# Block-causal attention with a gated feed-forward: low parts of q and k on another engine, scores and transposes in another order

## The chip, the cores and the metric

The kernel runs on one core of a Trainium2 chip. The metric is the device time of one execution in microseconds (us). Five engines work side by side, each through its own queue in order: TensorE (PE in the profile: matmuls and transposes, with weight loads shown as PEld), VectorE (DVE), ScalarE (ACT), GpSimd (POOL) and SyncE (SP, which issues DMAs).

## The reference

```python
def _attn_ref(q, k, v):                      # q, k, v: (8, 8, 576, 64)
    scores = scale * np.matmul(q, k.transpose(0, 1, 3, 2))
    mask = block_i >= block_j                # blocks of 64 positions
    scores = np.where(mask, scores, -1000000000.0)
    scores = scores - np.max(scores, axis=-1, keepdims=True)
    attn = np.exp(scores)
    attn = attn / (np.sum(attn, axis=-1, keepdims=True) + 1e-09)
    return np.matmul(attn, v)

def _moe_ref(x, w_in, g_ln, w_sg, b_sg, w_out):   # x: (8, 576, 512), the heads side by side
    h = gelu_tanh(x @ w_in)                  # w_in: 512 x 1024
    u, v = h[..., :512], h[..., 512:]
    v_n = (v - mean(v)) / np.sqrt(var(v) + 1e-06) * g_ln
    v_s = np.einsum('ts,bsd->btd', w_sg, v_n) + b_sg[None, :, None]
    return x + (u * v_s) @ w_out             # w_out: 512 x 512
```

Matmuls are made in near-fp32 precision from two parts of each operand, a high and a low one (`hi` is the value in the PE's shorter fp32 form, `lo` is the value less `hi`): hi x hi + hi x lo + lo x hi.

## The kernel before

The 64 heads of 8 batches are taken as 32 pairs. One *slot* (the function `slot`, lines 743 to 806) belongs to one pair n: it makes the attention values of pair n and, interleaved with them, the scores of pair n+1, so that the softmax of the next pair runs on DVE and ACT while PE does something else. Four slots make a batch.

In a slot PE does, in this order before the change: the transposes of the probabilities of pair n (tiles `pa`, `pb`, `pc`, `pd`, by the methods `turn0`, `turn2` with `turn2_rest`, `turn1` with `turn1_rest`, and `turn_first`), each two banks (one for each head) and each followed by a copy to SBUF as `pt` (by ACT or DVE); the score matmuls of pair n+1 in four steps (`step1` to `step4`, tile `s`, hereafter s1 to s4), each followed on DVE by a masked maximum of every row (`negm`; the instruction that applies the mask writes `prob` and accumulates the maximum) and on ACT by the exponentials (`exponents`); the matmuls of probabilities by values (`av0`, `av2`, `av1`, tile `ob`); and `turn_sums`, the transposes of the reciprocal sums `rx` to `pd` and `pe`, by which `normalise` multiplies (`x`). `split` cuts x into high and low parts (`xh` on DVE, `xl` and a tail on POOL). The reciprocal sums come from `inverse` at the head of a slot: `ri` on DVE, then `rx` on POOL.

In the seven places `hole(g[0])` to `hole(g[6])` of a slot stand *groups* of the feed-forward of an earlier batch: 5 of `accv`, 8 of `accu`, 8 of `accs` and 8 of `acco`, 29 for a batch, each one accumulation in one bank. Slots 0 to 3 have none, since no batch is complete. The table `FIRST` (line 741) says for slots 4 to 7 how many groups each place gets, `PLAN` (line 739) for all later slots.

PSUM has 8 banks in two pools, which are handed out in rotation: five for `s`, `ob` and the groups (`sbank`), three for the transposes (`pbank`). A tile can be written only when the reader of the bank's former tile is done: a `pa` follows the former `pd` or `pe`, a group follows an `s` that the maxima have read.

Inputs come a slot or two ahead. `load_qk` fetches q and k of pair n+2 by two DMAs; `split_qk` (lines 127 to 135), called near the end of slot n, cuts them in two: one cast on DVE (`qk_h`, 128x1152), then two subtractions on POOL (`qk_l`, 128x576 each). All these tiles have one buffer. Weights arrive as float64 and are made to high and low parts in small steps (`weight_step`; `load_weight`, lines 220 to 241, keeps `AHEAD` DMAs under way): each step has three operations on DVE (`w`), two on ACT and one on POOL (`wi_l`, `wo_l`). The table `WS` (line 731) says how many steps each of the slots 0 to 8 gets; a part that is needed earlier is pulled in by `need`.

Only PE's order is that of the program text inside slots. On the other engines the scheduler of the framework orders instructions by its own estimate when operands and buffers will be free, and each engine then works through that order.

The lines that the change touches are printed below with the functions that hold them.

Of the kernel before, what the change touches and what calls it, by code (L numbers as in the profile page):

```python
# [9 lines left out]
F32 = mybir.dt.float32  # L10
# [4 lines left out]
ALU = mybir.AluOpType  # L15
# [13 lines left out]
def kernel(  # L29
# [13 lines left out]
    B, H, D, S = qT.shape  # L43
    P = 128
    BLK = 64
    DM = H * D
# [22 lines left out]
    def page(dtype, n, name):  # L69
        tag, bufs = KINDS.get(name, KINDS["w"])  # L70
        return sp.tile([P, n], dtype, tag=tag, name=name, bufs=bufs)

    def bank(tag, name, bufs):
        return psum.tile([P, 512], F32, tag=tag, name=name, bufs=bufs)

    def sbank(name):
        return bank("s", name, 5)

    def pbank(name):
        return bank("p", name, 3)  # L80
# [22 lines left out]
    V, A, G, SP = Pinned(nc.vector, "V"), Pinned(nc.scalar, "A"), Pinned(nc.gpsimd, "G"), Pinned(nc.sync, "S")  # L103
# [23 lines left out]
    def split_qk(n):  # L127
        t = qk[n]
        hi = sp.tile([P, 2, S], F32R, tag="qk_h", name="qk_h", bufs=1)
        lo = sp.tile([P, 2, S], F32R, tag="qk_l", name="qk_l", bufs=1)  # L130
        V.tensor_copy(hi, t)
        for i in (1, 0):
            G.tensor_tensor(lo[:, i, :], t[:, i, :], hi[:, i, :].bitcast(F32), op=ALU.subtract)
        q_h, k_h, q_l, k_l = hi[:, 0, :], hi[:, 1, :], lo[:, 0, :], lo[:, 1, :]
        qk[n] = [(q_h, k_h), (q_h, k_l), (q_l, k_h)]

# [16 lines left out]
    t = sbank("warm")  # L153
# [15 lines left out]
    for s in (0, 1):  # L169
        t = cp.tile([P, NT, 2 * D], F32, name=f"v_f{s}")  # L170
# [5 lines left out]
    for s in range(4):  # L176
        row = []
        for i in range(NT):
            t = cp.tile([P, P * (i + 1) if i else BLK], F32, name=f"prob{s}_{i}")
# [8 lines left out]
    wo_h = cp.tile([P, NC, DM], F32R, name="wo_h")  # L188
    wo_l = cp.tile([P, NC, DM], F32R, name="wo_l")
# [5 lines left out]
    def split_weight(x, dh, dl):  # L195
        A.copy(dh, x)
        G.tensor_tensor(dl, x, dh.bitcast(F32), op=ALU.subtract)

    def from_f64(raw, dh, dl):

        n = raw.shape[-1]
        words = raw.bitcast(U32).rearrange("p (n t) -> p n t", t=2)
        hi, lo = words[:, :, 1], words[:, :, 0]
        tm = page(U32, 2 * n, "w")
        t, m = tm[:, :n], tm[:, n:]

        A.mul(m.bitcast(F32), hi.bitcast(F32), 2.0**-112)

        V.tensor_scalar(t, lo, 29, None, op0=ALU.logical_shift_right)
        V.scalar_tensor_tensor(
            t, hi, 0x80000000, t, op0=ALU.bitwise_and, op1=ALU.bitwise_or
        )
        V.scalar_tensor_tensor(
            t, m, 3, t, op0=ALU.logical_shift_left, op1=ALU.bitwise_or
        )
        split_weight(t.bitcast(F32), dh, dl)

    def load_weight(src, cols, dh, dl):  # L220

        W, AHEAD = 256, 4
        parts = [(c, slice(f, f + W)) for f in range(cols.start, cols.stop, W) for c in range(NC)]
        raws = {}

        def fetch(k):
            if k < len(parts):
                c, fs = parts[k]
                raws[k] = page(src.dtype, W, "raw")
                SP.dma_start(raws[k], src[c * P : (c + 1) * P, fs])  # L230

        for k in range(AHEAD):
            fetch(k)
        for k, (c, fs) in enumerate(parts):
            args = (raws.pop(k), dh[:, c, fs], dl[:, c, fs])
            if src.dtype == F32:
                split_weight(*args)
            else:
                from_f64(*args)
            fetch(k + AHEAD)  # L240
            yield True
# [26 lines left out]
    def load_gains():  # L268
# [10 lines left out]
            ("u0", load_weight(w_in, slice(0, DH // 2), wi_h, wi_l)),  # L279
            ("u2", load_weight(w_in, slice(DH // 2, DH), wi_h, wi_l)),  # L280
            ("s", load_spatial()),
            ("o", load_weight(w_out, slice(0, DM), wo_h, wo_l)),
        ]
    )

    def weight_step():

        with ExitStack() as stack:
            for ins in newest.values():
                stack.enter_context(tc.issue_after(ins.ins))  # L290
            while weights and next(weights[0][1], None) is None:
                weights.popleft()
# [96 lines left out]
    class Values:  # L389
# [15 lines left out]
            pt = self.pt[a, j] = sp.tile([P, 512], F32, tag="pt", name="pt", bufs=4)  # L405
            copy(TE[a, j], pt, t)

        def turn0(self, a):

            t = pbank("pa")  # L410
            for i in (4, 3, 2, 1):
                self.turn(a, t[:, (i - 1) * P : i * P], i, 0)
            self.out(a, 0, t)

        def turn2(self):

# [99 lines left out]
    def run_side(k):  # L516

        while k > 0 and side and side[0][0] != "G":
            k -= 1
            side.popleft()[1]()  # L520

    def run_gelu():

        if side and side[0][0] == "G":
            side.popleft()[1]()
# [196 lines left out]
    def hole(k=1):  # L722

        while k > 0 and work:
            try:
                next(work[0])
                k -= 1
            except StopIteration:
                work.popleft()

    WS = [2, 2, 2, 1, 10, 3, 3, 3, 2]

    def load_share(n, k):

        if n < len(WS):
            for _ in range(WS[n] * (k + 1) // 4 - WS[n] * k // 4):
                weight_step()

    PLAN = ["1111111", "1111111", "1111111", "1111112"]

    FIRST = ["1111111", "1111101", "0011011", "1011010"]

    def slot(n, sc):
        va = Values(n, sc)
        nx = Scores(n + 1) if n + 1 < N else None
        g = [int(x) for x in (FIRST if n // 4 == 1 else PLAN)[n % 4]]
        if n + 2 < N:
            load_qk(n + 2)
        if n + 1 < N:
            load_v(n + 1)  # L750
        va.inverse()
        va.turn0(0)
        va.turn0(1)
        hole(g[0])
        load_share(n, 0)
        run_side(2)

        va.turn2()
        va.turn2_rest()
        if nx:  # L760
            nx.step1()
            nx.step2()
        va.av0()
        if nx:
            nx.exponents(1, 4)
        hole(g[1])
        load_share(n, 1)
        run_side(2)
        hole(g[2])
        run_side(2)  # L770
        va.turn1()
        va.turn1_rest()
        va.turn_first()
        if nx:
            nx.step3()
            nx.step4()
        va.av2()
        if nx:
            nx.exponents(3, 0, 2)
        hole(g[3])  # L780
        load_share(n, 2)
        run_side(2)
        va.av1()
        va.av00()
        va.turn_sums()
        hole(g[4])
        va.normalise()

        wait = n // (H // 2) > 0 and n % (H // 2) < 2
        pending.append(va.split)  # L790
        if not wait:
            while pending:
                pending.popleft()()
        run_side(2)
        if n + 2 < N:
            split_qk(n + 2)
        load_share(n, 3)
        hole(g[5])
        run_gelu()
        run_side(3)  # L800
        hole(g[6])
        run_side(3)
        if n % (H // 2) == 1:
            while pending:
                pending.popleft()()
        return nx
# [75 lines left out]
```

## Time and profile before

| | before |
|---|---|
| three runs | 792.67, 793.02 and 795.04 us |
| profiled execution | 792.86 us, span 791.0 us |
| PE busy | 757.9 us (96%) |
| DVE busy | 495.5 us (63%) |
| ACT busy | 450.6 us (57%) |
| POOL busy | 272.4 us (34%) |
| mean granted PE clock | 0.985 |

The span is the time from the first to the last recorded instruction. A busy PE is not PE at its peak: the table of stretches further down also lists the granted clock, which is below full speed in the first 100 us. Rows of the timeline read: start, duration, engine, line, operation, written tile <- read tiles, shape, and, in brackets, the idle time of the engine before it with the instruction that ended it. Rows of the waits read: who waited for whom, total us, times, longest.

Where things lie: slot 0 starts at 10.6 us, slot 4 (the first with groups) at 70.9, slot 8 at 166.4, slot 9 at 192.3. From slot 8 on the four slots of a batch take 92.9 us.

### The profile page before, as it was taken

The page shows a single profiled execution, that of the slowest core. Times are in us where ns is not written, and L with a number is a line of the kernel's source. Part 1 is how long each engine was busy: PE and PEld are TensorE (multiplying, and loading weights), DVE is VectorE, ACT ScalarE, POOL GpSimd, SP SyncE. Part 2 cuts the span into 40 slices and gives each one's busy share as a digit, 9 for nine tenths or more (in the row PEclk, how much of TensorE's full clock was granted, in tenths as well). Part 3 has the DMA queues.
Part 4 walks back from the last instruction along what each step waited for, and adds up shares of the span by engine and source line. Part 5 has one row for each costly group of instructions (what it writes and reads, how often), then busy time and mean ns, then how long its engine had stood idle before and what let it go on. Part 6 is the DMA issues. An engine that isn't in the chain of part 4 may idle for free.

```text
span 791.0 us, 15794 instructions
## 1 busy us (share of the span) xinstructions
PE 757.9 (96%) x5926; PEld 640.4 (81%) x5926; DVE 495.5 (63%) x1457; ACT 450.6 (57%) x1172; POOL 272.4 (34%) x331
## 2 busy tenths in 40 slices
PE   7876998999999999999999999999999999999998
PEld 5554786878888888887888888888888978888998
DVE  5888679985866467654866548564676647633532
ACT  4775688567854478435973368544793358721600
POOL 4354265552424124351133414332243510422121
PEclk9989899999999999999999999999999999999999
DMA  7224324212241024311142122410233101320032
GB/s 231 70 92 145 96 91 140 88 61 75 76 150 61 1 76 121 106 60 38 39 136 90 61 75 61 132 65 31 76 107 120 60 7 71 105 76 31 1 120 75
DMA packets 46911, 65.66 MB, mean 83 GB/s; under 512 B 4082, under 2 KB 22514, under 8 KB 46836
## 3 DMA queue, kind: packets, MB, share of 16 engines
q1 hardware_dynamic: 46836, 64.67, 25.5%
q8 instruction: 46, 0.75, 0.4%
q14 instruction: 29, 0.24, 0.1%
HBM read 45.78 MB, written 18.87 MB: 82 GB/s over the span
## 4 chain that ended last, share of the span: by engine, by line
PE 77%; DVE 12%; ACT 8%; issue 1%; SPq 1%; DMA 1%; POOL 1%; DVEq 0%; POOLq 0%; ACTq 0%
PE accs L88 14%; PE acco L88 13%; PE accv L88 13%; PE ob L88 9%; PE s L88 8%; PE accu L88 8%; PE pc L91 3%; PE pb L91 3%; DVE bs L101 3%; ACT prob L101 3%; PE pa L91 2%; DVE w L101 2%; ACT L101 1%; DVE prob L101 1%; PE pe L91 1%; DVE pt L101 1%
## 5 line engine op out<-in xcount | busy, mean ns | idle before, releaser
L101 ACT ACTIVATE prob<-prob,negm 128x448 f32<-128x448 f32 (+4 forms) x320 | 176.3, 554 | 44.1 <-DVE negm L101 41.4
L101 POOL TENSOR_TENSOR qk_l<-qk_f,qk_h 128x576 fp32r<-128x576 f32 x62 | 91.9, 1502 | 231.6 <-issue 98.9
L101 DVE CUSTOM_DVE_ANT_0 prob<-s,mask 128x288 f32<-128x288 f32 (+2 forms) x320 | 117.0, 421 | 64.6 <-PE s L88 64.6
L88 PE MATMUL ob<-pt,v_f 128*64 128x512 f32 (+4 forms) x640 | 105.7, 443 | 0.9 <-ACT pt L101 0.8
L101 POOL TENSOR_TENSOR gl<-u,gh 128x288 fp32r<-128x288 f32 x64 | 51.8, 810 | 108.5 <-DVE gh L101 71.2
L88 PE MATMUL s<-qk_h 64*128 64x288 f32 (+1 forms) x372 | 87.4, 341 | 0.4 <-ACT u L101 0.4
L88 PE MATMUL accu<-xh,wi_h 128*128 128x288 f32 x256 | 78.1, 305 | 5.1 <-DVE negm L101 5.1
L88 PE MATMUL s<-qk_l,qk_h 64*128 64x288 f32 (+1 forms) x372 | 82.2, 302 | 0.0
L88 PE MATMUL accs<-ws_h,vh 128*128 128x288 f32 x256 | 78.2, 305 | 1.5 <-DVE negm L101 1.5
L88 PE MATMUL s<-qk_h,qk_l 64*128 64x288 f32 (+1 forms) x372 | 77.9, 299 | 0.0
L88 PE MATMUL acco<-gh,wo_h 128*128 128x288 f32 x256 | 77.7, 303 | 0.0
L88 PE MATMUL accs<-ws_h,vl 128*128 128x288 f32 x256 | 75.6, 295 | 0.0
L88 PE MATMUL accs<-ws_l,vh 128*128 128x288 f32 x256 | 75.5, 295 | 0.0
L88 PE MATMUL accu<-xl,wi_h 128*128 128x288 f32 x256 | 75.5, 295 | 0.0
L88 PE MATMUL accu<-xh,wi_l 128*128 128x288 f32 x256 | 75.4, 295 | 0.0
L88 PE MATMUL acco<-gl,wo_h 128*128 128x288 f32 x256 | 75.4, 294 | 0.0
L88 PE MATMUL acco<-gh,wo_l 128*128 128x288 f32 x256 | 75.4, 294 | 0.0
L88 PEld LDWEIGHTS ob<-pt,v_f 128*64 128x64 f32 x640 | 38.2, 137 | 42.0 <-issue 29.4
L88 PE MATMUL accv<-wi_h,xh 128*128 128x512 f32 x160 | 66.0, 413 | 3.8 <-POOL xh L101 3.8
L88 PEld LDWEIGHTS s<-qk_h 64*128 64x128 f32 x372 | 64.0, 188 | 1.4 <-ACT u L101 0.6
L101 DVE TENSOR_TENSOR u<-accs,u 128x288 f32<-128x288 f32 x64 | 29.2, 456 | 55.4 <-PE accs L88 55.3
L88 PEld LDWEIGHTS s<-qk_h,qk_l 64*128 64x128 f32 x372 | 63.8, 187 | 0.0
(104 smaller groups left out, 1954.6 us busy)
## 6 DMA issues: line engine op xcount, KB each, us to landing
spill<-x SPq DMA_DIRECT2D x32, 288.0 KB, 3.8
xr<-spill SPq DMA_DIRECT2D x32, 288.0 KB, 3.3
out_T<-xr SPq DMA_DIRECT2D x32, 288.0 KB, 3.3
qk_f<-in_qT SPq DMA_DIRECT2D x31, 288.0 KB, 3.2
qk_f<-in_kT SPq DMA_DIRECT2D x31, 288.0 KB, 3.8
v_f<-in_v SPq DMA_DIRECT2D x32, 256.0 KB, 3.1
raw<-in_w_in SPq DMA_DIRECT2D x16, 256.0 KB, 4.8
raw<-in_w_out SPq DMA_DIRECT2D x8, 256.0 KB, 4.8
```

The source lines that it names most:

```text
L88: return pin(nc.tensor.matmul(*a, **k), "P")
L91: return pin(nc.tensor.transpose(out, in_, identity), "P")
L101: return lambda *a, **k: pin(f(*a, **k), self.letter)
```

## The change

1. `split_qk`: the low parts are made on DVE, by one subtraction of 128x1152 instead of two of 128x576 on POOL.
2. `turn0`: both heads' `pa` tiles are taken together, and the transposes of block row 2 of both heads, which the exponentials finish last, come after those of block rows 4, 3 and 1.
3. In the first four slots (`early`), s1 and s2 and the first value matmuls (`av0`) come right behind `pa`, and `pb` (`turn2`) after them.
4. `turn1`, the whole-array transposes of `pc`, moves from behind the groups g[1] and g[2] to right behind `av0`; its small transposes (`turn1_rest`) stay.
5. `turn_sums` moves from the slot's end to right behind `av2`, ahead of the group g[3].
6. The tables: `WS` moves weight steps from slots 4, 6 and 7 to slots 5 and 8; `w_out` keeps 2 DMAs under way instead of 4; `FIRST` moves a group from the head of slot 4 to slot 5.

```diff
     hi = sp.tile([P, 2, S], F32R, tag="qk_h", name="qk_h", bufs=1)
     lo = sp.tile([P, 2, S], F32R, tag="qk_l", name="qk_l", bufs=1)
     V.tensor_copy(hi, t)
-    for i in (1, 0):
-        G.tensor_tensor(lo[:, i, :], t[:, i, :], hi[:, i, :].bitcast(F32), op=ALU.subtract)
+    V.tensor_tensor(lo, t, hi.bitcast(F32), op=ALU.subtract)
...
-    def load_weight(src, cols, dh, dl):
-        W, AHEAD = 256, 4
+    def load_weight(src, cols, dh, dl, AHEAD=4):
+        W = 256
...
-            ("o", load_weight(w_out, slice(0, DM), wo_h, wo_l)),
+            ("o", load_weight(w_out, slice(0, DM), wo_h, wo_l, 2)),
...
-        def turn0(self, a):
-            t = pbank("pa")
-            for i in (4, 3, 2, 1):
-                self.turn(a, t[:, (i - 1) * P : i * P], i, 0)
-            self.out(a, 0, t)
+        def turn0(self):
+            t = [pbank("pa"), pbank("pa")]
+            for tiles in ((4, 3, 1), (2,)):
+                for a in (0, 1):
+                    for i in tiles:
+                        self.turn(a, t[a][:, (i - 1) * P : i * P], i, 0)
+            for a in (0, 1):
+                self.out(a, 0, t[a])
...
-    WS = [2, 2, 2, 1, 10, 3, 3, 3, 2]
+    WS = [2, 2, 2, 1, 8, 5, 0, 0, 8]
...
-    FIRST = ["1111111", "1111101", "0011011", "1011010"]
+    FIRST = ["0111111", "1111111", "0011011", "1011010"]
...
-        va.turn0(0)
-        va.turn0(1)
+        va.turn0()
         hole(g[0])
...
-        va.turn2()
-        va.turn2_rest()
+        early = n < H // 2
+        if not early:
+            va.turn2()
+            va.turn2_rest()
         if nx:
             nx.step1()
             nx.step2()
         va.av0()
+        if early:
+            va.turn2()
+            va.turn2_rest()
         if nx:
             nx.exponents(1, 4)
+        va.turn1()
         hole(g[1])
...
         hole(g[2])
         run_side(2)
-        va.turn1()
         va.turn1_rest()
         va.turn_first()
...
         va.av2()
+        va.turn_sums()
         if nx:
             nx.exponents(3, 0, 2)
         hole(g[3])
...
         va.av1()
         va.av00()
-        va.turn_sums()
         hole(g[4])
         va.normalise()
```

Three places show what this does to the engines' orders. The first is PE in slot 0, from the first transposes on. In this piece of the difference the rows with - are those of before, those with + of the change (`prob_4` is block row 4 of the probabilities; the same sequence comes in slots 1 to 3).

```order
 L91 MATMUL pa<-ident,prob_4_116 128x128
 L91 MATMUL pa<-ident,prob_3_114 128x128
-L91 MATMUL pa<-ident,prob_2_112 128x128
 L91 MATMUL pa<-ident,prob_1_110 128x128
 L91 MATMUL pa<-ident,prob_4_125 128x128
 L91 MATMUL pa<-ident,prob_3_123 128x128
+L91 MATMUL pa<-ident,prob_1_119 128x128
+L91 MATMUL pa<-ident,prob_2_112 128x128
 L91 MATMUL pa<-ident,prob_2_121 128x128
-L91 MATMUL pa<-ident,prob_1_119 128x128
+L88 MATMUL s<-qk_h 128x288 x2
+L88 MATMUL s<-qk_l,qk_h 128x288 x2
```

Block row 2 of both heads moves to the end of `pa`, and the first score matmuls of the next pair follow at once, where ten `pb` transposes stood.

The second place is DVE between slots 0 and 1, from the cast of q and k (pair 2) to the first maxima of the next scores. Before:

```order
L101 CAST qk_h<-qk_f 128x1152
L101 TENSOR_SCALAR w<-raw 128x256
L101 SCALAR_TENSOR_TENSOR w<-raw,w 128x256
L101 TENSOR_TENSOR ri<-sums,tiny 128x10
L101 RECIPROCAL ri<-ri 128x10
L101 SCALAR_TENSOR_TENSOR w<-w 128x256
L101 TENSOR_TENSOR x<-pe,x 128x512
L101 TENSOR_TENSOR x<-pd,x 128x64
L101 CAST xh<-x 128x576
L101 COPY pt<-pa 128x512
L101 COPY pt<-pb 128x512
L101 ISA prob_4_116,negm<-s,mask 128x288
```

The same place after the change:

```order
L101 CAST qk_h<-qk_f 128x1152
L101 TENSOR_SCALAR w<-raw 128x256
L101 TENSOR_TENSOR qk_l<-qk_f,qk_h 128x1152
L101 SCALAR_TENSOR_TENSOR w<-raw,w 128x256
L101 TENSOR_TENSOR ri<-sums,tiny 128x10
L101 TENSOR_TENSOR x<-pe,x 128x512
L101 SCALAR_TENSOR_TENSOR w<-w 128x256
L101 TENSOR_TENSOR x<-pd,x 128x64
L101 RECIPROCAL ri<-ri 128x10
L101 CAST xh<-x 128x576
L101 COPY pt<-pa 128x512
L101 ISA prob_4_116,negm<-s,mask 128x288
```

`qk_l` stands third, ahead of the multiply by `pe`, and the copy of `pb` is no longer ahead of the first maxima.

The third place is PE in slot 9, around `av0` (the row `ob`). Before, then after the change:

```order
L88 MATMUL s<-qk_h,qk_l 128x288 x2
L88 MATMUL ob<-pt,v_f_105 64x512 x2
L88 MATMUL accu<-xh,wi_h 128x288
L88 MATMUL accu<-xl,wi_h 128x288
L88 MATMUL accu<-xh,wi_l 128x288
```

```order
L88 MATMUL ob<-pt,v_f_105 64x512 x2
L91 MATMUL pc<-ident,prob_4_134 128x128
L91 MATMUL pc<-ident,prob_3_132 128x128
L91 MATMUL pc<-ident,prob_2_130 128x128
L91 MATMUL pc<-ident,prob_4_143 128x128
L91 MATMUL pc<-ident,prob_3_141 128x128
L91 MATMUL pc<-ident,prob_2_139 128x128
L88 MATMUL accu<-xh,wi_h 128x288
```

Six whole-array transposes now stand between `ob` and the first matmul of the group; in the same way five (`pd`, four `pe`) stand between the `ob` of `av2` and the next group.

## The prediction

> **What bounds the kernel now.** The page comes first: which engine is busy, and at what clock.
>
> ```profile
> PE 757.9 (96%) x5926; PEld 640.4 (81%) x5926; DVE 495.5 (63%) x1457; ACT 450.6 (57%) x1172; POOL 272.4 (34%) x331
> PEclk9989899999999999999999999999999999999999
> ```
>
> TensorE (PE) is busy 757.9 of 791.0 us, and the diff leaves its matmuls and transposes the same in number. So an edit can win only from the 33.1 us in which PE stands still (and from clock), and can lose without limit. The second step is to see where the 33.1 us lie, with the busy time in stretches (after the span: PE, weight load, DVE, ACT, POOL, then granted clock, DMA share, GB/s).
>
> ```profile
> 0.00:20.00 20.00, 15.59 (x87) 11.48 (x88) 10.80 (x38) 9.37 (x27) 8.54 (x39) 0.91 0.70 232
> 20.00:40.00 20.00, 16.29 (x139) 11.13 (x138) 17.16 (x62) 15.04 (x48) 7.69 (x10) 0.91 0.21 66
> 40.00:60.00 20.00, 15.08 (x118) 10.27 (x114) 16.82 (x46) 13.54 (x45) 10.57 (x13) 0.83 0.33 99
> 60.00:80.00 20.00, 13.24 (x102) 9.38 (x103) 16.00 (x47) 11.16 (x34) 9.90 (x13) 0.89 0.44 141
> 80.00:100.00 20.00, 20.00 (x124) 14.64 (x124) 13.19 (x44) 13.48 (x38) 6.08 (x6) 0.85 0.26 89
> 100.00:120.00 20.00, 18.88 (x151) 16.14 (x151) 14.60 (x38) 16.97 (x37) 10.77 (x12) 1.00 0.29 90
> 120.00:140.00 20.00, 16.63 (x147) 13.40 (x143) 18.11 (x43) 17.87 (x44) 11.89 (x11) 1.00 0.43 139
> 140.00:160.00 20.00, 19.07 (x167) 16.13 (x165) 18.07 (x51) 11.12 (x35) 11.82 (x14) 1.00 0.29 86
> ```
>
> Of the idle time 19.8 us stand in the first 80 us (slots 0 to 3 and the opening of slot 4, where there are no feed-forward groups yet) and 5.4 us in 100 to 160 (slots 5 to 7). VectorE (DVE) is busy 80 to 86% from 20 to 80 us and 90% from 120 to 160, against 63% over the span. The third step is what ends PE's idle time, over the whole span:
>
> ```profile
> PE pa L91 <- ACT pt L101: 6.6, 4, 2.1
> PE accu L88 <- DVE negm L101: 5.1, 7, 0.7
> PE pa L91 <- ACT prob L101: 3.9, 4, 1.5
> PE accv L88 <- POOL xh L101: 3.8, 1, 3.8
> PE pb L91 <- DVE x L101: 3.3, 3, 1.2
> PE pb L91 <- DVE pt L101: 1.9, 1, 1.9
> ```
>
> The transposes pa and pb wait for copies, exponentials and the multiply x that empty their banks; the first accu group behind ob waits for the row maxima negm. The fourth step is what DVE does between two slots (end of slot 1), with POOL beside it in the last row:
>
> ```profile
> 40.27 0.75 DVE L101 CAST qk_h<-qk_f 128x1152 fp32r<-128x1152 f32 x1
> 40.94 0.28 DVE L101 TENSOR_SCALAR w<-raw 128x256 uint32<-128x256 uint32 x1
> 41.25 1.58 DVE L101 SCALAR_TENSOR_TENSOR w<-raw,w 128x256 uint32<-128x256 uint32 x1
> 42.76 1.36 DVE L101 TENSOR_TENSOR ri<-sums,tiny 128x10 f32<-128x10 f32 x1
> 44.56 0.69 DVE L101 TENSOR_TENSOR x<-pe,x 128x512 f32<-128x512 f32 x1
> 41.15 2.95 POOL L101 TENSOR_TENSOR qk_l<-qk_f,qk_h 128x576 fp32r<-128x576 f32 x2 [1.23 <-PE pe L91]
> ```
>
> A 128x10 add takes 1.36 us here and ends as POOL's second subtraction ends (42.76 + 1.36 against 41.15 + 2.95). DVE is held up by POOL's qk_l. The groups by shape say that this is the rule, not one case:
>
> ```profile
> L101 POOL TENSOR_TENSOR qk_l<-qk_f,qk_h 128x576 fp32r<-128x576 f32 x62 | 91.9, 1502 | 231.6 <-issue 98.9 <-DVE qk_h L101 69.8 <-PE accu L88 48.7
> L101 DVE TENSOR_TENSOR ri<-sums,tiny 128x10 f32<-128x10 f32 x32 | 24.3, 759 | 10.9 <-ACT prob L101 9.6 <-POOL qk_l L101 1.3
> L101 DVE TENSOR_TENSOR x<-pe,x 128x512 f32<-128x512 f32 x32 | 22.0, 688 | 19.6 <-PE pe L91 13.6 <-ACT x L101 6.0
> L101 DVE TENSOR_TENSOR x<-pd,x 128x64 f32<-128x64 f32 x32 | 6.9, 215 | 0.0
> ```
>
> The add costs 759 ns on average, although a multiply of 64 columns takes 215.
>
> **The change, part by part.**
>
> *Low parts on DVE.* POOL loses 62 operations, 91.9 us. DVE gets 31 of 128x1152, a size that the trace does not show on DVE with these operands. From 64 and 512 columns (215 and 688 ns) a column costs 473/448 = 1.06 ns, so one is 215 + 1088 x 1.06 = about 1.36 us, 42 us in all. Against that the holds go: ri falls from 759 ns to 215 at most, 0.54 x 32 = 17 us. In slot 1's boundary the exchange is better: there 1.58 + 1.36 of held time (of which some 0.6 would be work) gives way to 1.36, so DVE is 1.0 us shorter. Lower end of the new operation's price: 0.75, like the cast above; upper end: 1.36 plus one POOL operation of 1.5 us that might be in its way, as the 1502 ns row has it. I take 1.36, since POOL stands idle at that place in the early slots.
>
> A page warns of that upper end. The Trainium skill, SBUF — State Buffer, section "Who interferes with whom", says that a DVE instruction with two SBUF inputs contends with a GpSimd instruction that reads SBUF, and that the second to issue blocks until the first is done. The held add above agrees with it. By it the new qk_l, which has two SBUF inputs, stays exposed to POOL's remaining operations; if it met one each time, the 1.36 would be about 2.9, and the exchange in the early slots a loss of 0.5 us each instead of a gain of 1.0.
>
> In slots 9 to 31 none of this reaches PE, since a group and pb stand on PE between the cast and s1, and DVE has free time there (63% over the span). There I cost it at nothing; without that cover it would be up to 1.36 a slot.
>
> *Early order (slots 0 to 3) and turn0.* Before, s1 stands behind pb, pb behind a bank that x<-pe empties. The cast at 40.27 above, and these rows, give the path:
>
> ```profile
> 46.79 0.61 PE L88 MATMUL s<-qk_h 64*128 64x288 f32 x1
> 55.83 0.75 DVE L101 CAST qk_h<-qk_f 128x1152 fp32r<-128x1152 f32 x1
> 56.81 0.43 DVE L101 SCALAR_TENSOR_TENSOR w<-raw,w 128x256 uint32<-128x256 uint32 x1
> L101 DVE CAST xh<-x 128x576 fp32r<-128x576 f32 x32 | 22.8, 731 | 0.5
> L101 DVE COPY pt<-pa 128x512 f32<-128x512 f32 x32 | 21.9, 685 | 5.3 <-PE pa L91 5.0
> 202.20 1.02 PE L91 MATMUL pc<-ident,prob 128*128 128x128 f32 x7
> 202.96 0.30 PE L91 MATMUL pd<-ident,prob 64*64 64x64 f32 x2
> ```
>
> From cast to s1 it takes 6.5 us, from cast to cast 15.6. Now only pa stands ahead of s1, and the second pa bank is the one that x<-pe empties. Behind the cast (0.67 to the next issue) DVE has one scalar operation (0.31), qk_l (1.36), one weight operation that is not held (0.43, the row at 56.81), ri (0.2) and x<-pe (0.69): 3.7 us. Then comes the second half of pa, four transposes: at full clock seven take 0.76 in the last two rows, so four 0.43, and I allow 0.6 for a lower clock. s1 comes at 4.3 instead of 6.5, 2.2 us earlier. Not all stays. The cast xh (0.73) and the copy of pa (0.69) now fall behind that point, the copies of pb stand behind the maxima of s1 and s2, and pc, pd and with them s3 wait for these copies. I give back 0.8, and count 1.4 for each of the boundaries 0/1, 1/2 and 2/3, together **4.2**; in slot 0 itself the earlier s1 is used up by the later s3. The ends are 0 (all given back) and 3 x 2.2 = 6.6.
>
> *FIRST.* The accv group at the head of slot 4, which waited 3.8 us for xh, is moved to slot 5. Its work is kept, the wait goes. What is late next there is pb, behind x<-pe as three times before: 3.3/3, so about 1.0 remains. Gain **2.8**, with ends 0 and 3.8.
>
> *Slots 5 to 7.* Waits of PE between 90 and 165 us:
>
> ```profile
> PE pb L91 <- DVE pt L101: 1.9, 1, 1.9
> PE accs L88 <- DVE negm L101: 1.5, 2, 0.8
> PE accu L88 <- DVE negm L101: 0.7, 1, 0.7
> ```
>
> The last two, 2.2 us, are those of a group right behind ob, and go by the next part. The first comes from a DVE queue that is full (91% busy in 120 to 140); fewer w_out steps lie there now, while qk_l comes in. I take half, 0.9. Together **3.1**, ends 0 and 4.5. The w_out steps moved into slot 8 put about 1.1 us of DVE work each (0.28 + 0.43 + 0.43, after the rows at 40.94 and 56.81) into a slot with 15 of 20 us used, which fills it, but PE has groups in front of it there; I count 0, and up to 2 lost.
>
> *turn1 and turn_sums ahead of groups.* Behind 165 us PE has one wait left, six times, like this one in slot 9:
>
> ```profile
> PE accu L88 <- DVE negm L101: 4.3, 6, 0.7
> 197.10 1.08 PE L88 MATMUL ob<-pt,v_f 128*64 128x512 f32 x4
> 198.91 0.40 PE L88 MATMUL accu<-xh,wi_h 128*128 128x288 f32 x1 [0.72 <-DVE negm L101]
> ```
>
> The group needs a bank that negm empties. Now six whole pc transposes stand between ob and it. Seven take 0.76 (the rows at 202.20 and 202.96), so six 0.65, almost all of 0.72: 6 x 0.65 = **3.9**, ends 0 (pc itself waits for its banks) and 5.1 with the seams saved.
>
> **Sum**, against the profiled execution's own 792.86 (span 791.0 and 1.9 around it; 0.16 below the median of 793.02): 4.2 + 2.8 + 3.1 + 3.9 = 14.0, so **778.9 us**.
>
> **Rivals.**
>
> 1. *The early slots give nothing.* pa waits for x<-pe, pc and pd for the copies of pb, and these take the place of the waits removed; for it speaks that DVE is busier there (17.16 of 20) than PE (16.29), against it the 1.0 us that DVE itself loses. Then 4.2 and 2.8 go: **785.9**.
> 2. *The group behind ob still waits.* If pc waits for the copy of pb or negm itself slides, 3.9 and 2.2 are lost: **785.0**. Against it: in slot 9 the banks of pb are emptied before negm begins.
> 3. *The clock.* The clock is 0.85 in 80 to 100, where PE is busy all the time, and 1.00 behind. If shorter waits keep it full there, up to 20 x 0.15 = 3.0 us more go: **775.9**. For it speaks that the low figures end with the idle stretches; against it, that 120 to 140 has 3.4 us of idle time at 1.00, so the tie is loose. The Trainium skill, TensorE: Matmul & The Clock Gate, Part 1, has the array at half clock after an idle window of about 3.4 us. Here, by the table of waits, no idle piece but one is as long, and yet the clock is below 1 from the start; the trace bears the rule out only in part.
> 4. *Slower: DVE becomes the bound.* In most of slots 0 to 8 DVE is at 80 to 91%. If the holds do not go but move to other operations, each of nine slots carries 1.36 us more on the engine that ends last: 12.2 us, no early gain, and only 3.9 left: **801.2**. It decides once DVE's work in a slot exceeds the slot's period; for slot 1, 17.16/20 x 15.6 = 13.4 + 1.36 = 14.8 with the holds, 12.4 without them. So it is near only if the holds stay.
>
> That the change does not do what it says is ruled out for the place of the instructions, which the order shows; for the holds it is rival 4.
>
> **Chances.** Forecast (776 to 783) 0.52; rival 3 0.12; rival 1 0.14; rival 2 0.08; rival 4 0.14, split into 0.09 for all nine slots and 0.05 for some of them, which ends near the time of before. 0.3% (2.4 us) is about what a measurement of this kernel tells from no change. So faster has 0.52 + 0.12 + 0.14 + 0.08 = 0.86, within 0.3% 0.05, slower 0.09. The range takes in the ends of the terms and the first three rivals: the low end is 792.86 less the upper ends, 6.6 + 3.8 + 4.5 + 5.1 = 20.0, so 773; the high end is 788, two us above rival 1 for a slot 8 that is full. What it leaves out is rival 4.
>
> **What would show it.** In the profile after: ri's mean under 300 ns, and a DVE qk_l row of 31 at about 1.36 us; PE idle in the first 80 us well under 19.8, with no wait of accv for xh; cast to cast in slots 1 to 3 about 14 us, not 15.6; accu <- negm under 1 us in all. A qk_l mean above 2 us, or ri still above 700, would show the hold moved; pc or pd waiting for pt in the first slots would show rival 1; DVE above 95% in the stretches up to 190 us, rival 4. The prediction is wrong if PE's idle time falls by less than 5 us or if its busy time grows.

## The result, and the profile after

The change took 799.07 us (median of 4 runs, 798.32 to 800.04) against 793.35 us for the kernel before on the same chip: a ratio of 1.0074 with a 95% interval of 1.0052 to 1.0096, so 0.74% slower. 778.9 us had been predicted.

The first view is the page of the change: busy time by engine, and granted clock in 40 slices.

```profile
PE 763.0 (96%) x5926; PEld 640.0 (80%) x5926; DVE 500.8 (63%) x1488; ACT 452.1 (57%) x1172; POOL 178.2 (22%) x269
PEclk8898997899999999999999999999999999999999
```

POOL lost 94 us, and DVE, which took the work over, is only 5.3 us busier (500.8 against 495.5). Two rows of the groups by shape of the change say why:

```profile
L101 DVE TENSOR_TENSOR qk_l<-qk_f,qk_h 128x1152 fp32r<-128x1152 f32 x31 | 41.9, 1353 | 0.6
L101 DVE TENSOR_TENSOR ri<-sums,tiny 128x10 f32<-128x10 f32 x32 | 5.1, 161 | 1.6 <-ACT prob L101 1.6
```

The new operation costs 1353 ns, and `ri` fell from 759 to 161 ns. This part of the forecast stands. The stretches of 20 us of the change (span, then PE, weight load, DVE, ACT, POOL; granted clock, DMA share, GB/s) say where it went wrong:

```profile
0.00:20.00 20.00, 16.17 (x84) 10.85 (x85) 12.69 (x49) 10.48 (x32) 5.86 (x37) 0.83 0.75 236
20.00:40.00 20.00, 16.34 (x127) 11.24 (x128) 13.15 (x47) 13.51 (x42) 4.21 (x7) 0.83 0.20 61
40.00:60.00 20.00, 16.35 (x138) 10.46 (x136) 17.05 (x60) 15.04 (x48) 5.74 (x10) 0.91 0.39 121
60.00:80.00 20.00, 16.95 (x130) 11.20 (x127) 14.47 (x55) 12.05 (x37) 6.43 (x10) 0.83 0.51 164
...
120.00:140.00 20.00, 7.10 (x49) 4.59 (x47) 16.00 (x36) 12.69 (x24) 7.20 (x8) 0.71 0.15 46
140.00:160.00 20.00, 19.82 (x157) 17.45 (x157) 14.93 (x38) 8.02 (x22) 6.49 (x9) 0.87 0.19 60
```

From 120 to 140 us PE is busy 7.1 of 20 us, and before it was 16.63. The clock there is 0.71 and in the next stretch 0.87, where it was 1.00 before. The waits of PE over the whole span name the cause:

```profile
PE accs L88 <- ACT vh L101: 10.6, 1, 10.6
PE pa L91 <- DVE x L101: 6.9, 4, 2.7
PE s L88 <- ACT u L101: 2.7, 6, 0.5
PE pb L91 <- DVE pt L101: 2.3, 1, 2.3
PE pc L91 <- ACT pt L101: 2.3, 1, 2.3
```

The first row is one wait of 10.6 us, of the first `accs` group for `vh`, the normalised v of batch 0. It was not there before. The waits accu <- negm (5.1), accv <- xh (3.8) and pb <- x (3.3) have gone, but pa now waits 6.9 us for the multiply x, pc 2.3 us for a copy `pt`, and six waits of s for ACT's copy `u` are new. The prediction's own sign of being wrong is there: PE's busy time grew (763.0 against 757.9 us) and its idle time did not fall by 5 us (34.9 against 33.1).

By slots, from the first pa transpose of one slot to that of the next (us, from the traces; slots 1 to 3 together; before, slot 4 holds seven groups and slot 5 six, in the change the other way round):

| slot | 0 | 1 to 3 | 4 | 5 | 6 | 7 | 8 | 13 to 16 |
|---|---|---|---|---|---|---|---|---|
| before | 15.35 | 44.97 | 35.16 | 20.92 | 21.22 | 18.16 | 25.95 | 92.90 |
| change | 21.00 | 39.65 | 28.77 | 20.94 | 34.85 | 17.09 | 26.87 | 92.80 |

Slot 6 lost 13.6 us, slot 0 lost 5.7, slots 1 to 3 won 5.3, slot 4 won 6.4 with one group fewer, and a steady batch won 0.1. From slot 9 to the end it is 599.0 us against 598.7. In the early slots these differences are not those of the order alone, since the granted clock differed too: in slot 0 it was 0.89 before and 0.67 in the change, in slots 1 to 3 0.85 and 0.91.

### The profile page after: what moved, and what is told of

It is laid out like the page before. It is cut to its first block, busy times and chain, and to the rows that moved or that the text cites. A ratio compares the mean times of both kernels' runs of the same rounds, so it can differ in the third digit from the quotient of the medians.

```text
span 797.9 us, 15741 instructions
## 1 busy us (share of the span) xinstructions
PE 763.0 (96%) x5926; PEld 640.0 (80%) x5926; DVE 500.8 (63%) x1488; ACT 452.1 (57%) x1172; POOL 178.2 (22%) x269
## 5 line engine op out<-in xcount | busy, mean ns | idle before, releaser
L88 PE MATMUL ob<-pt,v_f 128*64 128x512 f32 (+4 forms) x640 | 108.4, 452 | 0.7 <-DVE vv L101 0.6
L88 PE MATMUL accs<-ws_h,vh 128*128 128x288 f32 x256 | 78.8, 308 | 10.6 <-ACT vh L101 10.6
L88 PE MATMUL s<-qk_h 64*128 64x288 f32 (+1 forms) x372 | 84.6, 340 | 2.7 <-ACT u L101 2.7
L88 PE MATMUL s<-qk_l,qk_h 64*128 64x288 f32 (+1 forms) x372 | 79.3, 301 | 0.0
L88 PE MATMUL s<-qk_h,qk_l 64*128 64x288 f32 (+1 forms) x372 | 74.3, 299 | 0.0
L88 PEld LDWEIGHTS ob<-pt,v_f 128*64 128x64 f32 x640 | 38.1, 138 | 42.5 <-issue 33.1
L101 DVE TENSOR_TENSOR xr<-acco,xr 128x288 f32<-128x288 f32 x64 | 29.3, 457 | 57.3 <-PE acco L88 47.1
L88 PEld LDWEIGHTS s<-qk_h 64*128 64x128 f32 x372 | 60.6, 186 | 5.0 <-ACT u L101 3.8
L88 PE MATMUL accv<-wi_l,xh 128*128 128x512 f32 x160 | 63.1, 394 | 0.0
```

The source lines that it names most:

```text
L88: return pin(nc.tensor.matmul(*a, **k), "P")
L101: return lambda *a, **k: pin(f(*a, **k), self.letter)
```

## The experiments

**1. Why v is late in slot 6.** The groups are drawn from generators. That of v puts its normalisation (GELU, batch statistics, scaling) into the list of side work only when the sixth group is drawn, since this stands in the code behind its fifth `yield`; and a slot starts a waiting GELU at one place, behind `hole(g[5])`. With FIRST of before the sixth group of slot 4 is drawn at g[5], just ahead of that place. With FIRST of the change it is drawn at g[6], behind it, and the side work goes into the program a slot later. That is theory A. Theory B puts the lateness down to the weight steps that WS moved. The trace of the change shows the chain:

```profile
119.07 4.03 DVE L101 CAST xh<-x 128x576 fp32r<-128x576 f32 x2 [2.44 <-PE accu L88]
126.43 0.76 DVE L101 TENSOR_TENSOR ws_l<-w,ws_l 1x576 fp32r<-1x576 f32 x1
127.20 0.69 DVE L101 BATCH_NORM_STATS2 bs<-vv 128x6 f32<-128x512 f32 x1
135.74 0.79 POOL L101 TENSOR_SCALAR rs<-stats 128x5 f32<-128x5 f32 x1 [0.91 <-DVE stats L101]
139.09 1.93 ACT L101 ACTIVATE vh<-vv,rs 128x512 fp32r<-128x512 f32 x3
139.85 0.61 PE L88 MATMUL accs<-ws_h,vh 128*128 128x288 f32 x1 [10.57 <-ACT vh L101]
```

The statistics stand in DVE's queue behind casts of xh, which wait for the last accu group, and behind a weight step. From the first of them to vh it takes 12 us, and PE, whose order is fixed, stands at the group that needs vh.

Four kernels tell the theories apart. The first, first_undone, is the change with FIRST of before:

```diff
-    FIRST = ["0111111", "1111111", "0011011", "1011010"]
+    FIRST = ["1111111", "1111101", "0011011", "1011010"]
```

> The change with FIRST of before (seven groups in slot 4 again, six in slot 5). Theory A (FIRST alone makes the late v chain: the sixth group of slot 4 is drawn one place later, behind the only point of the slot that starts the GELU of v, so GELU, moments and scaling of batch 0 are put into the program one slot later): the row accs <- ACT vh of 10.6 us falls under 1.5, the clock stays at 1.00 from 105 us on, a wait of accv for xh comes back in slot 4 (2 to 4 us), 786 to 790 us. Theory B (the spatial weight steps that WS moves into slot 5, with qk_l, fill DVE and POOL, and so v is late): the 10.6 stay, 797 to 801 us.

785.39 us (ratio to before 0.9910, interval 0.9885 to 0.9935). The second, gelu_early, is the change with its FIRST, but the GELU of v started once more in slot 4:

```diff
         hole(g[6])
+        if n == 4:
+            run_gelu()
+            run_side(3)
         run_side(3)
```

> The change with FIRST as it is, and in slot 4 alone one more call behind the last group that starts the GELU of v and three of its side steps. Theory A: wait of accs for vh under 1.5 us without the slot 4 wait coming back, batch statistics of batch 0 before 115 us instead of from 127.2, 784 to 788 us. Theory B: no difference, 797 to 801 us.

786.70 us (0.9912, 0.9885 to 0.9940). The third, ws_undone, is the change with the table WS of before:

```diff
-    WS = [2, 2, 2, 1, 8, 5, 0, 0, 8]
+    WS = [2, 2, 2, 1, 10, 3, 3, 3, 2]
```

> The change with the table WS of before (weight steps spread over slots 4 to 8; two DMAs ahead for w_out as in the change). Theory A: the wait of accs for vh stays, 8 to 12 us, 796 to 801 us. Theory B: it goes under 3 us, 785 to 790 us.

793.19 us (0.9993, 0.9979 to 1.0007). The fourth, before_first, is the kernel before with FIRST of the change alone (and two DMAs ahead for w_out):

> The kernel before with FIRST of the change and two DMAs ahead for w_out, all else as before. Theory A: the wait of accv in slot 4 (3.8 us) goes, a wait of accs for vh of 8 to 12 us comes in slot 6 with a stretch of half clock, 799 to 805 us. Theory B: only the gain, 788 to 792 us.

801.23 us (1.0104, 1.0084 to 1.0124). The batch statistics of batch 0 are one row in the view of the tile `bs` (count, ns, first and last start); before they ran from 105.9 to 110.9 us. In the change:

```profile
L101 DVE BATCH_NORM_STATS2 bs<-vv x5: 652/658/694, 127.2 to 134.3; 128x6 f32<-128x512 f32 x4, 64x6 f32<-64x512 f32 x1
```

In gelu_early:

```profile
L101 DVE BATCH_NORM_STATS2 bs<-vv x5: 651/664/695, 100.3 to 106.9; 128x6 f32<-128x512 f32 x4, 64x6 f32<-64x512 f32 x1
```

In before_first:

```profile
L101 DVE BATCH_NORM_STATS2 bs<-vv x5: 650/655/694, 125.1 to 132.5; 128x6 f32<-128x512 f32 x4, 64x6 f32<-64x512 f32 x1
```

They start at 97.2 us in first_undone and at 118.2 in ws_undone. Theory A holds: wherever FIRST has the group moved and the GELU is not started anew, the statistics come at 118 us or later and accs waits (9 to 11 us in all three), and in the kernel before the moved group alone costs 1.0%. gelu_early shows that it is the place of the start and not the moved group itself. One part of theory A's expectation missed: in first_undone no wait of accv for xh came back in slot 4. And B has a share: ws_undone missed both expectations (796 to 801 and 785 to 790 us). It still waits 9.3 us, but is 6 us faster than the change; 3.6 us of that are in slot 6 (31.26 against 34.85). One thing that differs is the two casts of xh ahead of the statistics: in the change they stand beside POOL's spatial weight step (`ws_l`, 119.51 to 121.14 us) and take 4.03 us, in ws_undone POOL's steps end at 117.57, before the casts, and these take 0.81. How the weight steps and the late chain add up there was not separated further.

**2. What each other part is worth, taken out of first_undone.** These four were timed on another chip than first_undone, so ratios to before are compared. The early order undone (order_undone):

```diff
-        early = n < H // 2
+        early = False
```

> FIRST as before (785.4 us in first_undone) and, of the change, the early order of slots 0 to 3 taken back: pb stands ahead of s1 there again. Theory C (the order itself brings the early gain of some 4 us): slot 4 starts at 70 to 71 us instead of 66.8, 788 to 791 us. Theory D (the gain there comes from DVE no longer being held by POOL): slot 4 starts before 68, 784 to 787 us.

787.31 us (0.9916, 0.9900 to 0.9932). qk_l back on POOL (pool_again):

```diff
-        V.tensor_tensor(lo, t, hi.bitcast(F32), op=ALU.subtract)
+        for i in (1, 0):
+            G.tensor_tensor(lo[:, i, :], t[:, i, :], hi[:, i, :].bitcast(F32), op=ALU.subtract)
```

> FIRST as before and qk_l back on POOL, the rest of the change kept. Theory C: under 2 us more than first_undone, 785 to 787.5 us. Theory D: ri back at some 700 ns or more, s1 behind qk_l of 3 us on POOL in slots 0 to 3, slot 4 starting 3 to 6 us later, 788 to 792 us.

800.25 us (1.0069, 1.0047 to 1.0090). turn1 and turn_sums at their old places (turns_undone):

```diff
-        va.turn1()
         hole(g[1])
...
+        va.turn1()
         va.turn1_rest()
...
-        va.turn_sums()
...
         va.av00()
+        va.turn_sums()
```

> FIRST as before and turn1 and turn_sums back at their old places. Theory E (in the steady slots the wait has only changed its name, from accu <- negm to s <- ACT u): the six waits of 0.7 come back and those of s <- ACT u go, batch period 92.9 against 92.8, within 1.5 us of first_undone, 784 to 787 us. The forecast's term (3.9 us in the steady slots): 788.5 to 791 us.

786.74 us (0.9904, 0.9881 to 0.9927). The weight steps of before (weights_undone):

```diff
-    WS = [2, 2, 2, 1, 8, 5, 0, 0, 8]
+    WS = [2, 2, 2, 1, 10, 3, 3, 3, 2]
...
-            ("o", load_weight(w_out, slice(0, DM), wo_h, wo_l, 2)),
+            ("o", load_weight(w_out, slice(0, DM), wo_h, wo_l)),
```

> FIRST, WS and the four DMAs ahead as before, the rest of the change kept. If the moved weight steps only cost (slots 8 and 9 were 1.5 us longer in the change): 783 to 785.5 us, slot 8 at 26.0 us instead of 26.9. If they are part of the gain (fewer steps in slots 6 and 7): 787 to 791 us, with waits back in slots 6 and 7.

785.76 us (0.9891, 0.9874 to 0.9908).

Only one of the four moves the time by more than these intervals, and it is the split: without it the rest of the change is slower than the kernel before. What the early order, the moved turn1 and turn_sums and the weight steps are worth inside first_undone lies below what these runs tell apart; order_undone (slot 4 at 68.9 us) and weights_undone (785.76 us) fell between their two expectations and decide nothing. Two rows of pool_again, from the waits of PE and from the groups by shape:

```profile
PE pa L91 <- DVE x L101: 15.4, 5, 5.4
```

```profile
L101 DVE TENSOR_TENSOR ri<-sums,tiny 128x10 f32<-128x10 f32 x32 | 23.5, 733 | 23.2 <-ACT prob L101 21.9 <-POOL qk_l L101 1.3
```

The holds are back, and pa, which in the new order stands ahead of s1, waits 15.4 us for the multiply x, which stands in DVE's queue behind the held add and the held weight operations. Its expectation, 788 to 792 us, was far too low.

**3. The split alone, and the rest on top of it.** The kernel before with nothing but this (split_alone):

```diff
-        for i in (1, 0):
-            G.tensor_tensor(lo[:, i, :], t[:, i, :], hi[:, i, :].bitcast(F32), op=ALU.subtract)
+        V.tensor_tensor(lo, t, hi.bitcast(F32), op=ALU.subtract)
```

> The kernel before with qk_l on DVE and nothing else of the change. Theory D (the relief of DVE from POOL's holds is the gain): ri at 200 ns or less, slots 0 to 3 some 1.5 to 2 us shorter each, slot 4 starting at 64 to 68.5 us instead of 70.9, 785 to 789 us. Theory C (it pays only together with the early order, since before it s1 waits for pb anyhow): 790.5 to 794 us.

782.11 us against 793.05 (0.9866, 0.9851 to 0.9881): faster than before and than the whole change, and below the 785 to 789 us expected. The clock does not explain it: on that chip the kernel before took 792.48 to 793.70 us in the six runs with a mean granted clock of 0.985, and split_alone 781.67 at 0.987. Its waits of PE, then its timeline at the end of slot 1, DVE and PE (in the trace of before the cast stands at 40.27 and s1 at 46.79):

```profile
PE pa L91 <- ACT pt L101: 6.6, 4, 2.1
PE accu L88 <- DVE negm L101: 5.0, 7, 0.7
PE pa L91 <- ACT prob L101: 4.6, 5, 1.5
```

```profile
37.34 0.75 DVE L101 CAST qk_h<-qk_f 128x1152 fp32r<-128x1152 f32 x1
38.21 1.34 DVE L101 TENSOR_TENSOR qk_l<-qk_f,qk_h 128x1152 fp32r<-128x1152 f32 x1
39.81 0.15 DVE L101 TENSOR_TENSOR ri<-sums,tiny 128x10 f32<-128x10 f32 x1
40.46 0.63 DVE L101 TENSOR_TENSOR x<-pe,x 128x512 f32<-128x512 f32 x1
41.96 0.39 PE L88 MATMUL s<-qk_h 64*128 64x288 f32 x1
```

From cast to x<-pe it takes 3.1 us instead of 4.3, and the wait of pb for x (3.3 us) is gone: s1 comes 4.6 us behind the cast instead of 6.5, without any new order. Slots 1 to 3 take 37.2 us instead of 45.0, but not all of that is waiting. The two rows are slots 1 to 3 of before and of split_alone (stretch, span, PE, weight load, DVE, ACT, POOL; granted clock, DMA share, GB/s):

```profile
25.92:70.89 44.97, 35.84 (x288) 24.93 (x286) 37.20 (x113) 30.12 (x96) 20.56 (x24) 0.85 0.32 103
26.04:63.27 37.23, 30.93 (x288) 22.21 (x286) 32.34 (x115) 28.22 (x92) 12.10 (x18) 0.95 0.39 125
```

PE's idle time falls by 2.8 us (9.1 to 6.3), about the wait of pb; its busy time falls by 4.9 at a higher granted clock. Slot 0 shows the opposite: 16.6 us at 0.69 against 15.4 at 0.89. So the slots are better taken together: slots 0 to 3 take 60.3 us before and 53.9 in split_alone, at 0.86 and 0.87.

Then parts of the change are put on top of it, each by its own lines of the diff shown with the change: the new turn0 (plus_turn0); the early order (plus_early); both (plus_both); turn1 and turn_sums moved (plus_turns).

> The kernel before with qk_l on DVE and the new turn0. Theory F (the new turn0 puts the second pa tile into the bank that x<-pe empties, so pa's wait for the copy pt turns into one for the multiply x, no shorter): pa <- ACT pt (6.6 us) goes, pa <- DVE x of 6 to 9 us comes, 782 to 785 us. If turn0 gains as the forecast has it: 779 to 781.5 us.

786.03 us (0.9919, 0.9904 to 0.9934).

> The kernel before with qk_l on DVE and the early order of slots 0 to 3, turn0 as before. Theory F: slot 0 grows to 19 us or more (s3 stands behind pc and pd, which wait for the copies of pb behind maxima and exponentials) and slots 1 to 3 stay at about 37 us in all, 783 to 786 us. If the order gains 1.4 us a boundary as forecast: 777 to 780 us.

787.10 us (0.9932, 0.9915 to 0.9950).

> The kernel before with qk_l on DVE, the early order and the new turn0. Theory F: no better than split_alone, 783 to 787 us. The forecast: 776 to 780 us.

785.21 us (0.9906, 0.9891 to 0.9922).

> The kernel before with qk_l on DVE, turn1 and turn_sums at their new places. Theory E (the steady wait changes its name): the batch period 92.8 against 92.9 us and 781 to 783.5 us. The forecast's 3.9 us: 777 to 779.5 us. If these moves cost in slots 1 to 3: 784 to 787 us.

784.71 us (0.9897, 0.9878 to 0.9916).

split_alone was timed on another chip than these four, so ratios to before are compared. It was timed once more later, on a third chip, at 0.9876 (0.9853 to 0.9899). turn0 and the early order each lie above both of its intervals and cost some 3 to 5 us on top of the split (0.9919 and 0.9932). Both together (0.9906) and plus_turns (0.9897) overlap with the second interval, so a loss there is not clear of the noise, but neither gains. plus_turns missed the forecast and the time of theory E (781 to 783.5 us), though the batch period of 92.8 us is as theory E has it. Slots 1 to 3 did not grow (37.3 us), but slot 6 did: it takes 23.1 us at a granted clock of 0.85, with a wait of pb of 3.2 us for a copy, against 20.6 us, 1.00 and 1.8 in split_alone; why was not followed up. The waits of PE in the first 80 us of plus_turn0:

```profile
PE pa L91 <- DVE x L101: 11.3, 4, 3.6
PE pa L91 <- ACT prob L101: 2.1, 3, 1.1
```

And of plus_early (whose profiled run, 792.05 us, lay at the top of its runs):

```profile
PE pa L91 <- ACT pt L101: 5.8, 4, 2.1
PE pc L91 <- ACT pt L101: 3.4, 1, 3.4
```

turn0 takes two banks at once, and the second is the one that x<-pe empties: 6.6 us of waiting for a copy became 11.3 of waiting for the multiply, and slots 1 to 3 took 43.7 us (at a granted clock of 0.84, against 0.95 in split_alone). With the early order pc in slot 0 waits 3.4 us for the copy of pb, which stands behind the exponentials of s1 and s2 on ACT; slot 0 took 19.5 us instead of 16.6. Here the clock is not the reason: it was 0.82 in this slot, against 0.69 in split_alone. Two kernels have the early order from slot 1 on (on top of first_undone): early_from_1, and early_from_1_ws, with weight steps moved from slot 8 to slot 7 besides:

```diff
-        early = n < H // 2
+        early = 0 < n < H // 2
```

> FIRST as before and the early order in slots 1 to 3 only, slot 0 in the old order. If the early order costs in slot 0 (19.5 to 21.0 us there against 16.5 in order_undone) and wins in 1 to 3 (37.5 against 43.1): slot 0 at about 16.5, slot 4 starting at 63 to 65 us, 781 to 784 us. If slots 1 to 3 are short only because slot 0 is long (the work is pushed from one to the other): slot 4 starting at 66 to 69, 785 to 788 us.

784.73 us (0.9903, 0.9886 to 0.9919), slot 0 at 16.5 as expected, but slots 1 to 3 at 42.1 instead of 37.5.

> The same with four of the weight steps of slot 8 moved to slot 7. If slot 8 is long because its DVE is full (26.9 us against 26.0 before): slot 8 back at 26.0 and slot 7 unchanged at 17.1, 0.5 to 1.5 us below early_from_1. If the steps only move the fill: slot 7 longer by as much, no difference beyond 0.5 us.

783.16 us (0.9882, 0.9862 to 0.9902), slot 8 at 26.3. So sparing slot 0 gave less than its 3 us: 2 came back in slot 1 in both (14.4 us against 12.4), and slots 2 and 3 took 27.7 in the one and 25.1 in the other, in one and the same order, at a granted clock of 0.88 and 1.00. Neither is faster than split_alone.

**4. Hold or earliness.** The split could win because DVE is no longer held, or because qk_l is ready sooner. One half on DVE, the other on POOL (half_split), makes one half of qk_l early and keeps a hold:

```diff
-        V.tensor_tensor(lo, t, hi.bitcast(F32), op=ALU.subtract)
+        for e, i in ((V, 1), (G, 0)):
+            e.tensor_tensor(lo[:, i, :], t[:, i, :], hi[:, i, :].bitcast(F32), op=ALU.subtract)
```

> The kernel before with the k half of qk_l on DVE and the q half on POOL. If holds of DVE are what the split removes: ri or a w operation beside POOL's subtraction is held for up to 1.4 us a slot, ri's mean 300 to 600 ns, and about half the gain goes, 785.5 to 790 us. If an earlier qk_l for s1 is the gain: 781 to 784 us as in split_alone.

787.22 us (0.9927, 0.9907 to 0.9947), beside split_alone once more on the same chip (split_again):

> split_alone once more, beside half_split and split_first on the same chip: 781 to 784 us, and the ratio to before within 0.3% of 0.9866.

782.72 us (0.9876, 0.9853 to 0.9899). From half_split the add in the groups by shape, and the timeline of DVE and POOL at the end of slot 0:

```profile
L101 DVE TENSOR_TENSOR ri<-sums,tiny 128x10 f32<-128x10 f32 x32 | 32.2, 1006 | 0.9 <-ACT prob L101 0.2
```

```profile
27.18 1.36 DVE L101 TENSOR_TENSOR ri<-sums,tiny 128x10 f32<-128x10 f32 x1
26.18 2.34 POOL L101 TENSOR_TENSOR qk_l<-qk_f,qk_h 128x576 fp32r<-128x576 f32 x1 [1.58 <-PE pd L91]
```

The add ends when POOL's subtraction ends (28.54 against 28.52), and 4.5 us of the gain are gone. Lateness of qk_l is not the reason: s1 starts at 30.55, 2 us after POOL's half is done, and PE waits for qk_l in none of the three traces (before, half_split, split_alone). What follows the time is DVE's chain up to x<-pe: from cast to x<-pe it takes 4.3 us before, 3.7 in half_split (25.30 to 28.99, at the end of slot 0) and 3.1 in split_alone, and the wait of pb for x is 3.3, 1.6 and 0 us. So the hold ahead of x<-pe is what the split removes. It delays POOL too: POOL's subtraction, issued with DVE's at 26.18, took 2.34 us, against a mean of 1.5 before. The mean of ri, 1006 ns, was above the 300 to 600 expected and even above that of before, so it shows that there is a hold, but not what the hold costs: before, weight operations ahead of the add were held as well (the 1.58 us in the rows of the prediction).

Last, the moved group with its GELU started in time, on top of the split (split_first: the diffs of first_undone, reversed, and of gelu_early, with two DMAs ahead for w_out):

> The kernel before with qk_l on DVE, FIRST of the change, two DMAs ahead for w_out, and in slot 4 the GELU of v and three side steps started behind the last group. If FIRST gains once the v chain is not late: the wait of accv for xh (1.7 us in split_alone) goes, 779.5 to 782 us. If that wait only moves: 782 to 785 us.

782.69 us (0.9860, 0.9839 to 0.9881). The wait of accv is gone and pb waits instead for a copy, 4.4 us once; no gain.

## Why the prediction was wrong

- **The price of the split: right.** 1.36 us for the new operation (measured 1.35), ri under 215 ns (161), no effect behind slot 9. What was too small is its worth. The forecast saw 1.0 us a slot in the exchange and gave the rest of the early gain to the new order. The split alone brings 10.9 us. In its profile slots 0 to 3 are 6.5 us shorter, slot 4 1.5 and slots 5 to 7 1.9, and slot 0 starts 1.2 us earlier. From slot 0 to slot 8 6.3 us of it is idle time of PE, of which the ended wait of pb for x is 3.3; besides the earlier start the rest is work of PE that ran faster, and whether the clock kept up because of the shorter waits was not shown.
- **FIRST: the step that failed most.** The forecast said of the moved group that "its work is kept, the wait goes", and counted 2.8 us. It asked only what stands behind the group on PE. The group's draw also sets when the program starts the normalisation of v, and that fell behind the one place that does so: the wait of 3.8 us went and one of 10.6 us came. Undone, the change gains 1.6% (1.0074 to 0.9910). No rival had this mechanism. That the slower rival forecast 801.2 us, near the 799.07 measured, is luck: it had DVE as the bound through holds that stay, but the holds went, and DVE was at 80% in the stretch that lost most, while PE waited for a chain, not for throughput.
- **The early order: wrong.** It was forecast to bring 1.4 us a boundary, 4.2 in all. On top of the split neither it nor the new turn0 gains, because s1 then waits for x<-pe by way of pa instead of pb, and pc for copies that stand behind maxima and exponentials. This is what rival 1 said. The forecast named both waits, gave back 0.8 us for them, and let slot 0 come out even; slot 0 lost 4 to 6 us, of which some 3 are the order's (19.3 us in turns_undone with it and 16.5 in order_undone without it, at a granted clock of 0.82 and 0.79).
- **The steady slots: wrong, the wait changed its name.** The six waits accu <- negm went as forecast, but a batch is 0.1 us shorter and not 0.65, and from slot 9 to the end nothing of the 3.9 us is left. Rival 2 had the loss, but by another way: it had the group itself still wait. The group behind `ob` still starts 6.6 us behind the slot's first pa, since pc only fills the wait; but s3 and s4 now follow the group without the whole-array transposes of pc between them, and s4 comes 0.7 us sooner to the bank that the group left. In slot 13 of the change, ACT and PE:

```profile
302.10 0.37 ACT L101 COPY u<-accu 128x288 f32<-128x288 f32 x1
302.39 0.72 ACT L101 ACTIVATE vn_t<-vv,rs 64x512 fp32r<-64x512 f32 x1
303.02 0.70 ACT L101 ACTIVATE vone<-vv,rs 64x512 fp32r<-64x512 f32 x1
303.63 0.37 ACT L101 COPY u<-accu 128x288 f32<-128x288 f32 x1
304.06 0.42 PE L88 MATMUL s<-qk_h 64*128 64x320 f32 x1 [0.45 <-ACT u L101]
```

The copy that empties the bank stands behind two scalings of v. From the first start of the score matmuls of s3 and s4 to the last it takes 2.09 us there, and 1.42 before, so the 0.7 is back; the row shows 0.45 of it as idle time.

- **Slots 5 to 7 and the clock.** Without FIRST these slots take 58.8 us instead of 60.3 (3.1 forecast), 58.4 with the split alone, so the split is enough for this gain. It is not always there: turns_undone, weights_undone and plus_turns have the split too and take 60.3 to 60.9 us, with a granted clock of 0.92, 0.85 and 0.85 in slot 6. The clock rival was right where it looked and wrong in the sum: from 80 to 100 us the clock is 1.00 in the change and was 0.85 before, but in the first 80 us it is 0.85 on average against 0.89, and in slot 6 0.76 against 1.00. From 131.8 to 145.3 us, inside the long wait and behind it, it is 0.50. A shorter stretch of 0.50, 125.0 to 128.2, lies ahead of that wait and stands in gelu_early too, which does not have the wait.
- **A slip in the sum.** The three rows of slots 5 to 7 hold 4.1 us and not the 4.5 of that term's upper end. It moves the low end of the range by 0.4 us and decides nothing.

## What to carry to other kernels

When a table moves a unit of work, follow what else the program does at the point where the unit is drawn: registration of later work, starts, pulls of operands. A wait on the critical engine is not the only thing that is moved.

Read the mean of a tiny operation against what its size should take. Here 759 ns for ten columns pointed at the only edit that is shown to pay; one such edit, made alone, is a better first experiment than the package around it.

Where a wait is for a shared buffer and is filled with other work of the same engine, look at the next buffer in the chain: here that one was not free earlier, and the wait came back under another name.

## What the runs showed of the hardware that was not expected

The granted clock in the first 80 us differs from one execution to the next. The change, gelu_early and first_undone have the same order of work on PE, DVE and ACT up to the last steps of slot 3, and yet slot 4 begins at 70.35, 70.33 and 66.75 us. The stretches of first_undone, to be read beside those of the change:

```profile
20.00:40.00 20.00, 15.81 (x135) 11.05 (x135) 13.97 (x52) 14.33 (x44) 4.69 (x7) 0.91 0.20 61
40.00:60.00 20.00, 16.09 (x145) 10.56 (x146) 18.06 (x63) 14.90 (x49) 7.30 (x12) 1.00 0.50 160
60.00:80.00 20.00, 16.36 (x124) 11.94 (x123) 15.23 (x51) 13.28 (x40) 5.31 (x8) 0.91 0.45 140
```

Its clock is 0.91, 1.00 and 0.91 where the change had 0.83, 0.91 and 0.83. So 3 to 4 us between two single profiles of the early slots mean nothing by themselves, which is as much as several of the edits above are apart, and the runs of one kernel spread as far (gelu_early from 783.62 to 787.84). The cause of a low clock stayed open. In the Trainium skill, TensorE: Matmul & The Clock Gate, Part 1, half clock comes after an idle window of about 3.4 us. No single wait of PE in these 80 us was longer than 2.7 us in the change, and the clock was below 1 all the same.
